# Moving half of the convolutions next to the next first product, and building the band matrices on TensorE, in a fused convolution and three-product kernel

## The chip, the cores and the metric

The kernel runs on one core of a Trainium2 chip. The metric is the device time of one execution in microseconds (us), taken as the median over several runs; less is better. Before the change it is 532.6 us (three runs, 532.53 to 532.73). One more execution was taken with the hardware profiler; all durations below that belong to single instructions come from it.

## The reference

A causal convolution over the sequence, with seven taps and one set of softmax weights for each of eight heads, feeds a gated product with four weight matrices:

```
# x: (8, 3904, 192), weight: (8, 7)
w = exp(weight - max) / (sum + 1e-9)            # softmax over the 7 taps of a head
x_pad = 6 rows of zeros, then x                 # for each of the 8 sequences
conv[b, s, h, :] = sum_k w[h, k] * x_pad[b, s + k, h, :]     # 24 columns a head
x2 = conv.reshape(31232, 192)
a, b = x2 @ w1, x2 @ w2                         # 192 x 1024 each
out = ((a * b) @ w3) @ w_out                    # 1024 x 1024, 1024 x 192
```

Since nothing stands between the last two products, the kernel multiplies w3 by w_out once (1024 x 192) and uses that as the weight of its second product.

## The kernel before

The 31232 tokens are two streams of 15616 tokens (`NS = 2`, index r). A stream is worked off in 31 rounds of 512 tokens (`CH`, `NR`), the last of 256.

**Convolution.** Tokens are cut into windows of 64 rows, which give 58 results each (`Q`, `ST`), and windows into ten blocks of 10 to 36 windows (`SIZES`). `load_x` brings a block's rows to the tile xb by DMA from GpSimd's queue, stream 0 on partitions 0 to 63 and stream 1 on 64 to 127. The convolution of a head is a product with a 64 x 64 band matrix whose seven diagonals hold the head's weights. `conv(b, h0, nh)` (L237) issues four matmuls of 64 x 64 tiles for each head (two halves of the block, two streams) into a PSUM buffer (tile cps, L254) and then moves the result to the tile convo (L271, or L428 in the prologue). `conv_two` (L480) calls it for two heads one by one, and after the last head of a block calls `store`, which writes convo to a scratch tensor in DRAM (rows, from SP's queue); `send` then issues transposing DMAs from rows to xT, also on SP. xT is a ring of four rounds. The first three blocks do not go through DRAM: TensorE transposes them (`pe_transpose`, tile tps, L307).

**Band matrices.** `band_of` takes the matrix of a head from the tile Aband, [128, 2, 2, 2, 64]: two groups g of four heads, a direct and a swapped half, two heads, 64 columns. Each needs its values on the partitions of either stream. Before the change, `band(g)` (L204) builds them on VectorE: a mask cmask with a one at every place of each of eight diagonals, made by GpSimd (L151), times the weights wsb (L206), then three additions that sum over the eight (L213 twice, L216); `band_swap` (L219) copies the two partition halves crosswise with VectorE and ScalarE.

**First product.** `first_product(R)` (L345) goes over eight column tiles ft of the 1024 columns. For each, six matmuls for a (pa) and six for b (pb), in pairs that use either half of the rows of the array (L360); ScalarE copies pa to asb (L366) and VectorE multiplies asb by pb into the tile abT (L367). Because x of the two streams lies on either partition half, the weights are needed on both halves: wn as loaded (`load_w`, in two column parts) and wsw with the halves exchanged (`swap_w`, L334, three column parts `WC`: 0 to 511, 512 to 767, 768 to 1023). Column tiles 0 to 3 use part 0, 4 and 5 part 1, 6 and 7 part 2.

**Second product.** `second_product(R, r)` (L372) has 32 matmuls of 128 x 192 (tile ops, L378); ScalarE empties it (osb, L383) and SP sends it to the output.

**Order.** The order on every engine is the one in which the code issues (`manual_schedule`). All PSUM tiles come in turn from four buffers of two banks each (tag banks), so a tile waits until the tile four before it has been emptied. The prologue (L425 to L462) makes the bands, the convolution of block 0 and its transposes, and the swapped weights. Then come the first products of rounds 0, 1 and 2 with the convolutions of blocks 1 and 2 in between (L470 to L478), the product of w3 and w_out with block 3 (L491), and the steady phases (L507). Phase p runs the first products of two rounds (phase 0: none), and the second products of two earlier rounds, `done` and `done + 1`, r = 0 and r = 1 each. A block has two phases; in each, `conv_two` runs twice, once between the two second products of each round, with both evictions on VectorE. GpSimd reloads x for the next block inside the phase, behind a small copy (pace) that waits for a first product. `warm` (L171) issues matmuls on zeros at the start.

Of the kernel before, what the change touches and what calls it, by code (L numbers as in the profile page):

```python
# [8 lines left out]

FP32 = mybir.dt.float32  # L10
BF16 = mybir.dt.bfloat16
AX = mybir.AxisListType
ALU = mybir.AluOpType
# [4 lines left out]
def kernel(  # L18
# [10 lines left out]
    nc = tc.nc  # L29

    B, S, D = x.shape
    H, K = weight.shape
# [1 line left out]
    DFF = moe_w1.shape[1]  # L34
    JT = DFF // 128
    PAD = K - 1
    KP = 8
    assert K <= KP

    NS = 2  # L40
    TS = B * S // NS
# [4 lines left out]
    Q = 64  # L46
# [7 lines left out]
    NB = len(SIZES)  # L54
# [14 lines left out]
    def banks(name):  # L69
        return psum.tile([128, NS, CH], FP32, tag="banks", name=name)  # L70
# [4 lines left out]
    def slot(shape, dtype, name):  # L75
        return stage.tile(shape, dtype, tag="slot", bufs=5, name=name)
# [68 lines left out]

    ones = const.tile([128, 1], BF16)
    nc.gpsimd.memset(ones, 1.0)
    cmask = const.tile([128, Q, KP], BF16)
    for r in range(NS):
        ps = slice(Q * r, Q * r + Q)  # L150
        nc.gpsimd.affine_select(  # L151
            out=cmask[ps], in_=ones[ps].unsqueeze(2).to_broadcast([Q, Q, KP]),
            pattern=[[-1, Q], [-1, KP]], compare_op=ALU.is_equal,
            fill=0.0, base=0, channel_multiplier=1)
    wn = [const.tile([128, DFF], BF16, name=f"wn{k}", tag=f"wn{k}") for k in range(3)]
    wsw = [const.tile([128, DFF], BF16, name=f"ws{k}", tag=f"ws{k}") for k in range(3)]

# [2 lines left out]
    def load_w(c0, c1):  # L160
        cs = slice(c0, c1)
        nc.gpsimd.dma_start(out=wn[0][:, cs], in_=moe_w1[0:128, cs])
        nc.gpsimd.dma_start(out=wn[2][0:Q, cs], in_=moe_w1[128:192, cs])
        nc.gpsimd.dma_start(out=wn[2][Q:128, cs], in_=moe_w2[128:192, cs])
        nc.gpsimd.dma_start(out=wn[1][:, cs], in_=moe_w2[0:128, cs])

    load_w(0, WC[2])
    ident = const.tile([128, 128], BF16)
    make_identity(nc, ident)

    def warm(n, t=None):  # L171
        t = banks("warm") if t is None else t
        for j in range(n):
            nc.tensor.matmul(t[:, j % 2, :], zeros[:, 0:128], zeros, start=True, stop=True)  # L174

    warm(28)


    wmax = const.tile([128, H], FP32)
    wsum = const.tile([128, H], FP32)  # L180
    wsb = const.tile([128, 2, 2, KP], BF16)
    nc.vector.memset(wsb, 0.0)  # L182
    nc.vector.reduce_max(out=wmax, in_=wall, axis=AX.X)
    nc.vector.tensor_tensor(
        out=wall, in0=wall, in1=wmax.unsqueeze(2).to_broadcast([128, H, K]), op=ALU.subtract)
# [3 lines left out]
    for r in range(NS):  # L189
        ps = slice(Q * r, Q * r + Q)  # L190
        nc.vector.tensor_tensor(
            out=wsb[ps, :, :, 0:K],
            in0=wall[ps].rearrange("p (g a e) k -> p g a e k", g=2, a=2)[:, :, r],
            in1=wsum[ps].rearrange("p (g a e) -> p g a e", g=2, a=2)[:, :, r].unsqueeze(3)
                .to_broadcast([Q, 2, 2, K]),
            op=ALU.mult)
# [4 lines left out]
        g, j, e = h // 4, (h % 4) // 2, h % 2  # L201
        return Aband[Q * r:Q * r + Q, g, int(j != r), e, :]

    def band(g):  # L204
        c = slot([128, 2, Q, KP], BF16, "cprod")
        nc.vector.tensor_tensor(  # L206
            out=c,
            in0=cmask.unsqueeze(1).to_broadcast([128, 2, Q, KP]),
            in1=wsb[:, g].unsqueeze(2).to_broadcast([128, 2, Q, KP]),
            op=ALU.mult)  # L210
        n = KP // 2
        while n > 1:
            nc.vector.tensor_tensor(out=c[:, :, :, 0:n], in0=c[:, :, :, 0:n],  # L213
                                    in1=c[:, :, :, n:2 * n], op=ALU.add)
            n //= 2
        nc.vector.tensor_tensor(out=Aband[:, g, 0], in0=c[:, :, :, 0], in1=c[:, :, :, 1],  # L216
                                op=ALU.add)

    def band_swap(g, half, f):  # L219
        d, e = ((Q, 0), (0, Q))[half]  # L220
        f(out=Aband[d:d + Q, g, 1], in_=Aband[e:e + Q, g, 0])


    xT = [const.tile([128, RING], BF16, name=f"xT{k}", tag=f"xT{k}") for k in range(NP)]
# [12 lines left out]
    def conv(b, h0, nh, evict=None, lead=0):  # L237
        n = SIZES[b] // 2
        if h0 == 0:
            convo_of[b] = work.tile([128, n, NP, NS, Q], BF16, tag="convo", bufs=2, name="convo")  # L240
        convo = convo_of[b]
        cps = banks("cps")
        warm(lead, cps)
        wd = nh * G

        def view(ps, r):
            return cps[ps, r, 0:n * wd].rearrange("p (w g) -> p w g", g=wd)

        for j in range(nh):
            h = h0 + j  # L250
            for c in range(2):
                xb, w0 = xb_of[b][c]
                for r in range(NS):
                    nc.tensor.matmul(  # L254
                        view(slice(Q * c, Q * c + Q), r)[:, :, j * G:(j + 1) * G],
                        band_of(h, r),
                        xb[Q * r:Q * r + Q, w0:w0 + n, h * G:(h + 1) * G],
                        start=True, stop=True)
        src = cps[:, :, 0:n * wd].rearrange("p r (w g) -> p r w g", g=wd)
        o, moves = 0, []  # L260
        for k, c0, m in segments(h0 * G, wd):
            moves.append((convo[:, :, k, :, c0:c0 + m].rearrange("p w r g -> p r w g"),
                          src[:, :, :, o:o + m]))
            o += m
        if h0 + nh == H:
            del xb_of[b]
        if evict == ():
            return moves
        for e, (dst, part) in enumerate(moves):
            f = evict or [nc.scalar.copy]  # L270
            f[e % len(f)](out=dst, in_=part)  # L271
# [28 lines left out]
    def pe_transpose(b, k, lead=0):  # L300
        n = SIZES[b] // 2
        convo = convo_of[b]
        tps = banks_bf16("tps")
        for w in range(lead):
            nc.tensor.transpose(out=tps[:, w % 2, :], in_=zeros[:, 0:128], identity=ident)
        for w in range(n):
            nc.tensor.transpose(  # L307
                out=tps[:, w, :],
                in_=convo[:, w, k].rearrange("p r g -> p (r g)"), identity=ident)
        t0 = tok(FIRST[b])  # L310
        dst = xT[k][:, t0:t0 + 2 * n * ST].rearrange("p (c w s) -> p c w s", c=2, w=n)
        src = tps[:, 0:n, :].rearrange("p w (c s) -> p c w s", c=2)
        return dst, src[:, :, :, 0:ST]
# [20 lines left out]
    def swap_w(k, part, engines):  # L334
        cs = slice(WC[part], WC[part + 1])
        for f, (d, e) in zip(engines, ((0, Q), (Q, 0))):
            f(out=wsw[k][d:d + Q, cs], in_=wn[k][e:e + Q, cs])
# [89 lines left out]
    def move(f, pair):  # L427
        f(out=pair[0], in_=pair[1])  # L428

    band(0)  # L430
    band_swap(0, 0, V)
    band_swap(0, 1, A)
    band(1)
    band_swap(1, 0, V)
    m0, m1 = conv(0, 0, 4, ())
    move(A, m0)
    band_swap(1, 1, A)
    move(V, m1)
    t0 = pe_transpose(0, 0, 10)
    swap_w(0, 0, (V, A))  # L440
    for m in conv(0, 4, 2, ()):
        move(V, m)
    for m in conv(0, 6, 2, ()):
        move(A, m)
    move(V, t0)
    swap_w(2, 0, (V, A))
    t1 = pe_transpose(0, 1, 8)
    move(V, t1)
    t2 = pe_transpose(0, 2)
    move(A, t2)  # L450
    swap_w(1, 0, (V, A))
    for k in (0, 2, 1):
        swap_w(k, 1, (P, V))
    load_w(WC[2], WC[3])
    load_x(2)
    for k in (0, 2, 1):
        swap_w(k, 2, (P, P))
    load_wo()
# [5 lines left out]
    def seq(*fs):  # L464
        def run():
            for f, *a in fs:
                f(*a)
        return run

    first_product(0, lead=2, between={  # L470
        2: seq((conv, 1, 0, 4)),
        3: seq((conv, 1, 4, 4)),
        6: seq((pe_transposes, 1))})
    first_product(1, {
        0: seq((conv, 2, 0, 4)),
# [4 lines left out]
    def conv_two(b, h, engines):  # L480
        for j, f in enumerate(engines):
            conv(b, h + j, 1, (f,))
        if h + 2 == H:
            store(b)

    def send(last):
        while sent[0] <= last and min((sent[0] + 1) * CH, TS) <= stored[0]:
            transposes(sent[0])
            sent[0] += 1
# [16 lines left out]
    done = 0  # L506
    for p, rounds in enumerate(phases):  # L507
        b, e = PROLOGUE_BLOCKS + p // 2, p % 2
        if b < NB:
            for xb, r, w in zero_rows.pop(b, []):  # L510
                nc.gpsimd.memset(xb[Q * r:Q * r + PAD, w, :], 0.0)
        for j, R in enumerate(rounds):
            first_product(R)
            if j == 0 and b + 1 < NB:
                P(out=pace, in_=abT_of[R][0:1, JT - 1, 1, 0:2])  # L515
                load_x(b + 1, (0, 1) if p == 1 else (e,))
        last = NR if p == len(phases) - 1 else done + 2
        for i in range(done, last):
            second_product(i, 0)
            if b < NB and i < done + 2:  # L520
                conv_two(b, 4 * e + 2 * (i - done), (V, V))
            second_product(i, 1)
        done = last
        send(min(NR - 1, LAG + 2 * p + 4))
    assert sent[0] == NR

# [29 lines left out]
```

## Time and profile before

| what | us |
|---|---|
| median of 3 runs | 532.6 |
| the profiled execution | 533.68 |
| its span on the core, first to last instruction | 532.0 |
| first matmul of the first product | 14.02 |
| all abT multiplies (L367), 248 of them | 298.4 |
| all copies to asb (L366) | 247.6 |
| all conv evictions on VectorE (L271), 65 | 52.0 |
| GpSimd busy in the whole span | 53.0 |

A line of the chain of waits has a start, a length and the instructions on it: it is followed back from the last instruction to whatever released each step. In a line of the timeline or of the groups, "x" is the number of instructions, the times are start and length (timeline) or the union and the mean of one (groups), and the brackets hold the idle time before and what ended it. PE is TensorE, PEld its weight loads, DVE VectorE, ACT ScalarE, POOL GpSimd, SP SyncE. A matmul's own length is modelled and overlaps with the next one's, so the distance between starts is what a matmul costs.

### The profile page before, as it was taken

How to read it: one execution, taken by the hardware profiler on the slowest of the kernel's cores; microseconds unless marked ns; L12 is line 12 of the kernel's file. 1: busy time of each engine (PE TensorE's matmuls, PEld its weight loads, DVE VectorE, ACT ScalarE, POOL GpSimd, SP SyncE). 2: the span in 40 equal slices, each digit the busy share in tenths (PEclk: the TensorE clock that was granted, in tenths of full speed). 3: DMA queues.
4: the chain of work that ended last, by engine and by line, in shares of the span. 5: the costliest groups of instructions: out<-in, count | busy, mean ns of one | idle time of the engine just before them, and what ended most of it. 6: DMA issues, size and time to landing. Idle time of an engine off the chain costs nothing.

```text
span 532.0 us, 12708 instructions
## 1 busy us (share of the span) xinstructions
PE 524.0 (98%) x5469; PEld 339.3 (64%) x5469; DVE 363.1 (68%) x350; ACT 317.4 (60%) x350; POOL 53.0 (10%) x95
## 2 busy tenths in 40 slices
PE   8999999999999999999999999999999999999995
PEld 4455874846658476584765757557575674847685
DVE  6779459578594875949669496784957849286560
ACT  3888647375573755737467374664746647375552
POOL 8851002002010100201001010020000000000000
PEclk9999999999999999999999999999999999999998
DMA  7999457989473694637956468655624065240203
GB/s 101 141 206 182 93 96 171 206 175 125 132 99 99 154 144 129 88 103 156 137 139 78 130 150 128 118 66 145 136 80 120 1 172 106 90 76 31 90 22 130
DMA packets 130541, 63.13 MB, mean 119 GB/s; under 512 B 83352, under 2 KB 129460, under 8 KB 130484
## 3 DMA queue, kind: packets, MB, share of 16 engines
q1 hardware_dynamic: 91764, 45.65, 35.7%
q0 software_dynamic: 38576, 16.63, 26.3%
q8 instruction: 43, 0.70, 0.6%
q14 instruction: 14, 0.11, 0.1%
q10 hardware_dynamic: 144, 0.03, 0.0%
HBM read 33.28 MB, written 34.82 MB: 128 GB/s over the span
## 4 chain that ended last, share of the span: by engine, by line
PE 94%; DVE 3%; ACT 1%; DMA 1%; issue 0%; ACTq 0%; DVEq 0%
PE ops L378 31%; PE pa L360 30%; PE pb L360 29%; PE cps L254 2%; DVE abT L367 1%; PE wps L418 1%; ACT asb L366 1%; DMA wall<-in_weight_dram 1%; PE tps L307 1%; PE w3ps L409 0%; DVE cprod L213 0%; DVE cprod L206 0%; DVE Aband L216 0%; DVE convo L428 0%; DVE w3T L412 0%
## 5 line engine op out<-in xcount | busy, mean ns | idle before, releaser
L367 DVE TENSOR_TENSOR abT<-asb,pb 128x1024 bf16<-128x1024 bf16 (+1 forms) x248 | 298.4, 1204 | 77.0 <-ACT asb L366 60.5
L366 ACT CAST asb<-pa 128x1024 bf16<-128x1024 f32 (+1 forms) x248 | 247.6, 999 | 64.1 <-PE pa L360 63.4
L360 PE MATMUL pb<-xT,wn 64*128 64x512 bf16 (+1 forms) x744 | 199.7, 373 | 0.2
L360 PE MATMUL pa<-xT,wn 64*128 64x512 bf16 (+1 forms) x744 | 197.8, 373 | 0.4
L360 PE MATMUL pa<-xT,ws 64*128 64x512 bf16 (+1 forms) x744 | 197.9, 373 | 0.0
L360 PE MATMUL pb<-xT,ws 64*128 64x512 bf16 (+1 forms) x744 | 195.7, 373 | 0.0
L360 PEld LDWEIGHTS <-wn 64*128 64x128 bf16 x1488 | 138.3, 94 | 84.6 <-issue 2.6
L360 PEld LDWEIGHTS <-ws 64*128 64x128 bf16 x1488 | 130.3, 94 | 72.0 <-issue 1.4
L378 PEld LDWEIGHTS <-abT 128*128 128x128 bf16 x1952 | 159.1, 98 | 13.8 <-issue 13.8
L378 PE MATMUL ops<-W_sb,abT 128*128 128x192 bf16 x1952 | 167.8, 246 | 0.0
L383 ACT COPY osb<-ops 128x768 f32<-128x768 f32 (+1 forms) x62 | 48.9, 789 | 134.1 <-PE ops L378 134.1
L271 DVE CAST convo<-cps 128x864 bf16<-128x864 f32 (+7 forms) x65 | 52.0, 847 | 66.7 <-PE cps L254 66.7
L111 POOL DMA_DIRECT2D xb<-in_x_dram x38 | 29.9, 797 | 12.2 <-DMA w3b<-in_moe_w_dram 5.2
L515 POOL COPY pace<-abT 1x2 bf16<-1x2 bf16 x9 | 1.6, 176 | 269.7 <-DVE abT L367 269.7
L254 PE MATMUL cps<-xb,Aband 64*64 64x432 bf16 (+3 forms) x320 | 17.8, 309 | 0.2 <-DVE abT L367 0.2
L174 PE MATMUL warm<-zeros 128*128 128x512 bf16 x28 | 8.9, 491 | 1.4 <-DVE wsb L182 1.4
L254 PEld LDWEIGHTS <-Aband 64*64 64x64 bf16 x320 | 5.8, 105 | 6.8 <-issue 5.7
L271 ACT CAST convo<-cps 128x640 bf16<-128x640 f32 (+4 forms) x13 | 7.4, 606 | 0.8 <-PE cps L254 0.8
L174 PEld LDWEIGHTS <-zeros 128*128 128x128 bf16 x30 | 3.4, 119 | 6.5 <-issue 3.6
L418 PE MATMUL wps<-wo_b,w3T 128*128 128x192 bf16 x64 | 6.3, 246 | 0.1
L418 PEld LDWEIGHTS <-w3T 128*128 128x128 bf16 x64 | 5.1, 98 | 1.0 <-issue 1.0
L409 PE MATMUL w3ps<-ident,w3b 128*128 128x128 bf16 x64 | 4.6, 219 | 0.0
(55 smaller groups left out, 64.3 us busy)
## 6 DMA issues: line engine op xcount, KB each, us to landing
out_dram<-osb SPq DMA_DIRECT2D x60, 384.0 KB, 2.9
xb<-in_x_dram POOLq DMA_DIRECT2D x14, 432.0 KB, 8.9
rows<-convo SPq DMA_DIRECT2D x7, 648.0 KB, 7.5
xb<-in_x_dram POOLq DMA_DIRECT2D x8, 384.0 KB, 9.9
w3b<-in_moe_w_dram POOLq DMA_DIRECT2D x8, 256.0 KB, 8.8
rows<-convo SPq DMA_DIRECT2D x3, 576.0 KB, 8.4
xT<-rows SPq DMA_TRANSPOSE x84, 2.7
rows<-convo SPq DMA_DIRECT2D x2, 540.0 KB
```

Source lines behind the costliest of these rows:

```text
L111: nc.gpsimd.dma_start(out=xb[Q * r:Q * r + Q, w:w + m, :], in_=x_spans(r, i, m))
L174: nc.tensor.matmul(t[:, j % 2, :], zeros[:, 0:128], zeros, start=True, stop=True)
L254: nc.tensor.matmul(view(slice(Q * c, Q * c + Q), r)[:, :, j * G:(j + 1) * G], band_of(h, r), xb[Q * r:Q * r + Q, w0:w0 + n, h * G:(h + 1) ...
L271: f[e % len(f)](out=dst, in_=part)
L307: nc.tensor.transpose(out=tps[:, w, :], in_=convo[:, w, k].rearrange("p r g -> p (r g)"), identity=ident)
L360: nc.tensor.matmul(p[:, r, 0:N], w_of(i, k, r)[rs, ft * 128:(ft + 1) * 128], xT[k][rs, r0:r0 + N], start=(k == 0), stop=(k == NP - 1))
L366: nc.scalar.copy(out=asb[:, :, 0:N], in_=pa[:, :, 0:N])
L367: nc.vector.tensor_tensor(out=ab[:, ft, :, 0:N], in0=asb[:, :, 0:N], in1=pb[:, :, 0:N], op=ALU.mult)
L378: nc.tensor.matmul(ops[:, g // 2, (g % 2) * D:(g % 2) * D + D], ab[:, jt, r, g * 128:(g + 1) * 128], W_sb[:, jt, :], start=(jt == 0), stop ...
L383: nc.scalar.copy(out=osb.rearrange("p (a g) d -> p a (g d)", g=2), in_=ops[:, 0:ng // 2, 0:2 * D])
L409: nc.tensor.transpose(out=tps[:, gt, :], in_=w3b[:, gt * 128:(gt + 1) * 128], identity=ident)
L418: nc.tensor.matmul(wps[:, 0, 0:D], w3T[:, gt, :], wo_b[:, gt, :], start=(gt == 0), stop=(gt == JT - 1))
```

## The change

Three edits go together.

In the steady phases, `conv_two` stays between the two second products of the first of the two rounds; the other call goes behind all four second products, directly ahead of the next phase's first product. The last phases, which have no block left, are as before.

The bands are made in another way. GpSimd makes a plain identity with 64 further columns that continue it (identw: columns 64 to 191 are an identity with its halves exchanged), and one diagonal strip of 70 columns on each partition half (diag) in place of cmask. `band_taps(g)` multiplies seven overlapping views of the strip, each shifted by one column, by the weights, one multiply on VectorE with the columns innermost; `band_sum(g)` sums the seven on TensorE, with the identity for the direct and the exchanged identity for the swapped half, and one copy from PSUM fills Aband[:, g]. wsb has seven entries in place of eight and is no longer cleared first.

The prologue is reordered: 18 warm matmuls in place of 28; no dummy transposes; convs of two heads; `swap_w` of part 0 for k = 0 and 2, and of parts 1 and 2 for all three, by GpSimd alone (before: part 0 by VectorE and ScalarE, part 1 by GpSimd and VectorE, part 2 by GpSimd); `load_w` of columns 768 to 1023 and `load_x(2)` between the swaps. In round 0 the second conv of block 1 goes from behind column tile 3 to behind column tile 4.

```diff
-    cmask = const.tile([128, Q, KP], BF16)
-    for r in range(NS):
-        ps = slice(Q * r, Q * r + Q)
+    identw = const.tile([128, 128 + Q], BF16)
+    diag = const.tile([128, Q + PAD], BF16)
+    for m in (identw[:, 0:128], identw[:, 128:128 + Q], diag[0:Q], diag[Q:128]):
+        p, n = m.shape
         nc.gpsimd.affine_select(
-            out=cmask[ps], in_=ones[ps].unsqueeze(2).to_broadcast([Q, Q, KP]),
-            pattern=[[-1, Q], [-1, KP]], compare_op=ALU.is_equal,
-            fill=0.0, base=0, channel_multiplier=1)
+            out=m, in_=ones[0:p].to_broadcast([p, n]), pattern=[[-1, n]],
+            compare_op=ALU.is_equal, fill=0.0, base=0, channel_multiplier=1)
+    ident, swapped = identw[:, 0:128], identw[:, Q:Q + 128]
...
-    ident = const.tile([128, 128], BF16)
-    make_identity(nc, ident)
...
-    warm(28)
+    warm(18)
...
-    wsb = const.tile([128, 2, 2, KP], BF16)
-    nc.vector.memset(wsb, 0.0)
+    wsb = const.tile([128, 2, 2, K], BF16)
...
-    def band(g):
...
-    def band_swap(g, half, f):
...
+    d0 = diag[:, 0:1]
+    taps = bass.AP(tensor=d0.tensor, offset=d0.offset,
+                   ap=[list(d0.ap[0]), [0, 2], [1, K], [1, Q]])
+
+    def band_taps(g):
+        c = slot([128, 2, K, Q], BF16, "cprod")
+        nc.vector.tensor_tensor(
+            out=c, in0=taps, in1=wsb[:, g].unsqueeze(3).to_broadcast([128, 2, K, Q]),
+            op=ALU.mult)
+        return c
+
+    def band_sum(g, c, f):
+        bps = banks("bps")
+        for v, lhsT in enumerate((ident, swapped)):
+            out = bps[:, 0, v * 128:v * 128 + 128].rearrange("p (e s) -> p e s", e=2)
+            for k in range(K):
+                nc.tensor.matmul(out, lhsT, c[:, :, k, :], start=(k == 0), stop=(k == K - 1))
+        f(out=Aband[:, g].rearrange("p v e s -> p (v e s)"), in_=bps[:, 0, 0:256])
...
-    band(0)
-    band_swap(0, 0, V)
-    band_swap(0, 1, A)
-    band(1)
-    band_swap(1, 0, V)
-    m0, m1 = conv(0, 0, 4, ())
-    move(A, m0)
-    band_swap(1, 1, A)
-    move(V, m1)
-    t0 = pe_transpose(0, 0, 10)
-    swap_w(0, 0, (V, A))
-    for m in conv(0, 4, 2, ()):
-        move(V, m)
-    for m in conv(0, 6, 2, ()):
-        move(A, m)
-    move(V, t0)
-    swap_w(2, 0, (V, A))
-    t1 = pe_transpose(0, 1, 8)
-    move(V, t1)
-    t2 = pe_transpose(0, 2)
-    move(A, t2)
+    c0, c1 = band_taps(0), band_taps(1)
+    band_sum(0, c0, A)
+    band_sum(1, c1, V)
+    for h, f in ((0, V), (2, A), (4, V), (6, A)):
+        for m in conv(0, h, 2, ()):
+            move(f, m)
+    swap_w(0, 0, (P, P))
+    swap_w(2, 0, (P, P))
+    load_w(WC[2], WC[3])
+    for k, f in ((0, V), (1, A), (2, V)):
+        move(f, pe_transpose(0, k))
     swap_w(1, 0, (V, A))
+    load_x(2)
     for k in (0, 2, 1):
-        swap_w(k, 1, (P, V))
-    load_w(WC[2], WC[3])
-    load_x(2)
+        swap_w(k, 1, (P, P))
     for k in (0, 2, 1):
         swap_w(k, 2, (P, P))
...
         2: seq((conv, 1, 0, 4)),
-        3: seq((conv, 1, 4, 4)),
+        4: seq((conv, 1, 4, 4)),
...
             second_product(i, 0)
-            if b < NB and i < done + 2:
-                conv_two(b, 4 * e + 2 * (i - done), (V, V))
+            if b < NB and i == done:
+                conv_two(b, 4 * e, (V, V))
             second_product(i, 1)
         done = last
+        if b < NB:
+            conv_two(b, 4 * e + 2, (V, V))
         send(min(NR - 1, LAG + 2 * p + 4))
```

Here V, A and P are copies by VectorE, ScalarE and GpSimd, and `move` empties one PSUM piece.

More of the change, by code (lines that the diff above doesn't have):

```diff
@@ L6 @@
 from concourse import bass_utils, mybir
-from concourse.masks import make_identity
 from concourse._compat import with_exitstack
@@ L36 @@
     PAD = K - 1
-    KP = 8
-    assert K <= KP
     NS = 2
@@ L191 @@
         nc.vector.tensor_tensor(
-            out=wsb[ps, :, :, 0:K],
+            out=wsb[ps],
             in0=wall[ps].rearrange("p (g a e) k -> p g a e k", g=2, a=2)[:, :, r],
@@ L202, in band_of @@
         return Aband[Q * r:Q * r + Q, g, int(j != r), e, :]
-    def band(g):
-        c = slot([128, 2, Q, KP], BF16, "cprod")
+    d0 = diag[:, 0:1]
[3 more added lines that the diff above has]
+        c = slot([128, 2, K, Q], BF16, "cprod")
         nc.vector.tensor_tensor(
-            out=c,
-            in0=cmask.unsqueeze(1).to_broadcast([128, 2, Q, KP]),
-            in1=wsb[:, g].unsqueeze(2).to_broadcast([128, 2, Q, KP]),
+            out=c, in0=taps, in1=wsb[:, g].unsqueeze(3).to_broadcast([128, 2, K, Q]),
             op=ALU.mult)
[L211 to L217, printed above, removed]
-    def band_swap(g, half, f):
-        d, e = ((Q, 0), (0, Q))[half]
-        f(out=Aband[d:d + Q, g, 1], in_=Aband[e:e + Q, g, 0])
+        return c
[6 more added lines that the diff above has]
+        f(out=Aband[:, g].rearrange("p v e s -> p (v e s)"), in_=bps[:, 0, 0:256])
     xT = [const.tile([128, RING], BF16, name=f"xT{k}", tag=f"xT{k}") for k in range(NP)]
```

## The prediction

> **What bounds the kernel now.** I read the page's busy shares and chain shares first, then the chain of waits in order of time at the start and in one steady phase, then the timeline of the other engines at those places.
>
> ```profile
> PE 524.0 (98%) x5469; PEld 339.3 (64%) x5469; DVE 363.1 (68%) x350; ACT 317.4 (60%) x350; POOL 53.0 (10%) x95
> PE 94%; DVE 3%; ACT 1%; DMA 1%; issue 0%; ACTq 0%; DVEq 0%
> ```
>
> TensorE holds 94% of the chain that ends last. So a change pays in two ways only: it lets the first real product start earlier, or it takes time out of TensorE's own row of work. The chain at the start (start us, length us, what):
>
> ```profile
> 6.74 0.70 DVE cprod L206
> ...
> 9.00 0.83 DVE cprod L206
> ...
> 10.74 0.64 DVE Aband L216
> ...
> 11.63 0.49 DVE convo L428
> ...
> 12.90 0.76 PE tps L307 x10
> 13.65 0.43 PE pa L174 x2
> 14.09 0.75 PE pa L360 x6
> 14.84 1.01 PE pb L360 x6
> ```
>
> VectorE builds both bands (6.74 to 11.60) while TensorE spins on zeros; the first product starts at 14.09, and its first pb takes 1.01 instead of the 0.65 of every later one, because ScalarE is still copying swapped weights. One steady phase:
>
> ```profile
> 94.34 0.65 PE pb L360 x6
> 94.99 2.75 PE ops L378 x32
> 97.73 0.49 PE cps L254 x8
> 98.22 5.39 PE ops L378 x64
> 103.61 0.49 PE cps L254 x8
> 104.10 2.75 PE ops L378 x32
> 106.84 0.75 PE pa L360 x6
> ```
>
> Nothing but TensorE is in it. 32 ops matmuls that follow their own kind take 2.64 (the piece at 62.41 of the same chain); behind a first product or a conv they take 2.75, and 64 take 5.39, which is 5.28 + 0.11. Six pa after pb take 0.65, after ops 0.75. Each change of kind costs 0.10 to 0.11. The timeline around it has the evictions:
>
> ```profile
> 97.77 0.80 ACT L383 COPY osb<-ops 128x768 f32<-128x768 f32 x1 [2.38 <-PE ops L378]
> 98.09 2.09 DVE L271 CAST convo<-cps 128x864 bf16<-128x864 f32 x3 [1.44 <-PE cps L254]
> 103.97 2.02 DVE L271 CAST convo<-cps 128x864 bf16<-128x864 f32 x2 [3.79 <-PE cps L254]
> ```
>
> VectorE empties two convs in 2.0 to 2.1 us, behind second products that don't need it. GpSimd at the start:
>
> ```profile
> 4.25 2.21 POOL L151 TENSOR_SCALAR_AFFINE_SELECT cmask<-ones 64x512 bf16<-64x512 bf16 x2
> ...
> 17.13 2.65 POOL L337 COPY ws<-wn 64x256 bf16<-64x256 bf16 x6 [0.45 <-DMA wn<-in_moe_w_dram]
> ```
>
> **The steady phases.** In the twelve phases that have a conv (p = 0 to 11) the second conv_two goes behind the last second product, against the next first product. Before, from the first ops to the end of the first pa: 2.75 + 0.49 + 5.39 + 0.49 + 2.75 + 0.75 = 12.62. After: 2.75 + 0.49 + 0.11 + 3 x 2.64 + 0.49 + pa. A pa behind a conv took 0.75 where it didn't wait (chain, 20.66) and 0.82 where it did (18.85). With 0.75 the sum is 12.51: one change of kind fewer, 0.11 a phase, 1.3 in twelve. With 0.82 it is 0.04 a phase, 0.5.
>
> What hid the moved evictions is gone: they now stand on VectorE ahead of the next abT multiply. Counted from the first conv matmul's start (97.66 in the timeline), they end 2.52 later (98.09 + 2.09). The four PSUM buffers go round as ops, ops, cps, cps, pa, pb, pa, pb, so the second pb takes the second cps. It wants to start at 0.56 + 0.75 + 0.65 + 0.65 = 2.61. The first abT could start when ScalarE's copy of the first pa ends, 0.56 + 0.75 + 1.01 = 2.32, and now starts at about 2.55 and ends at 3.77 (1.22 each); the third pb, which needs its buffer, starts at 3.91. The cover holds by about 0.1 us, and grows, since abT takes 1.22 to 1.24 and a pa with pb 1.295. The first pb needs the last osb gone: 0.9 against 1.31. I take off 0.1 in all for phases whose evictions come in three pieces: **1.2**. Ends 0 (0.1 lost in every phase) and 1.3.
>
> On SP, store moves behind the out of the last second product, so rows are written about 2.6 us later and the transposes behind them too. They were issued at 114.43 (x6, 9.9 us) for rounds that start at 139.5: 15 us of cover; without it the 2.6 would show in full, once per block. On GpSimd nothing waits for the moved conv but the reload of its xb, a phase later.
>
> **The prologue.** wsb is ready at 6.64 as before (the memset of wsb was off the path, at 1.28). Removed on VectorE: two L206 (0.69, 0.82), four L213 (0.43, 0.41 twice), two L216 (0.38, 0.63), two swaps (0.19). Added: two taps multiplies of 896 elements each, which the trace doesn't show. Ends: by L206 (1024 in 0.69, both operands contiguous) 0.61; by abT (1024 in 1.22, the slowest full multiply) 1.07. The weight is now one value held for 64 elements; L216, whose operands aren't contiguous either, takes 0.51 for 128, far worse per element than L206. So I take 1.07: taps at 6.74 to 7.83 and 7.86 to 8.95.
>
> The Trainium skill, "Vector Engine (DVE) Microarchitecture Reference", section 5.1, speaks against this multiply: two 16-bit results a cycle need an innermost step of one, and one element read again and again by a two-source operation ran at one a cycle. By it the multiply is an estimated 0.93 plus a fixed part, by L206 alone 0.61, which would bring the sum below 0.28 earlier.
>
> TensorE: 18 warm matmuls instead of 28. They start 0.427 apart up to 6.49 and 0.216 apart from 6.85 on, so the eighteenth starts at 7.71 and band_sum(0) can start at 7.93. Its 14 matmuls of 128 columns, by w3ps (8 in 0.45), take 0.056 each: last start 8.65, done at 8.87. Band_sum(1) waits for the taps, 9.0 to 9.95. ScalarE empties the first (256 columns, by 320 in 0.43: 0.38), VectorE the second (by 320 in 0.49: 0.41), done at 10.38. Convs of two heads start at 9.88, 10.0, 10.42 and 10.5, done 0.33 later. xb landed early: the convs before ran at 10.18 straight off the warm matmuls.
> VectorE: heads 0-1 (480 columns, 0.66) to 11.07, heads 4-5 (0.49 + 0.31) to 11.85. ScalarE: heads 2-3 (0.30 + 0.43) to 11.07, heads 6-7 (0.56) to 11.66. Transposes at 11.15, 11.65 and 11.92, five each. Moves to xT: VectorE 0.44 to 12.30, ScalarE 0.64 to 12.76, VectorE to 12.84. Two warm matmuls (0.43) fit in between; pa starts at 12.62 against 14.02 of its first matmul. ScalarE's half of ws1 (0.62) ends at 13.40, so pb still waits 0.16, and the second pa starts at 13.9 instead of 15.48: **1.55**. Ends 0.6 (0.1 more at each of ten hand-overs) and 1.85 (taps at 0.61).
>
> GpSimd: four selects of 128, 64, 70 and 70 elements replace two of 512 (1.08 each) and the later identity (0.20 + 0.29). By the identity's 0.29 for 128 they take about 0.95, so the four weight loads issue 1.2 earlier (5.2 instead of 6.41), land near 8.9 to 11.4, and x of block 1 goes out at 7.45. It takes over four 64x512 copies: no row, 0.40 to 0.80 by 64x256, I take 0.80. They run from 9.0 to 12.3; the last operand of the first pa needs them at 13.06. Then the second loads and x of block 2 issue (3.8, to 16.1), against 16.7 before; six 64x256 copies (2.65) to 18.75, six more to 21.4. Their readers come at 18.35 (fifth pa; its pb, which reads the last copied, 19.0) and 21.4 to 22.05. Cover 0.3 to 0.7 us. Output weights and w3 leave 1.7 later; the last w3 landed at 36.0 and is used past 50.
>
> Conv (1, 4..7) goes from behind the fourth pa/pb to behind the fifth. Same pieces, and the waits of 0.1 to 0.2 that follow each conv in these rounds stay: 0, ends -0.2 and 0.2.
>
> **Sum.** 1.2 + 1.55 = 2.75. The profiled execution took 533.68 (span 532.0), 1.1 above the median 532.6; I take the difference off the median: **529.85 us**, and 530.9 for an execution like the profiled one. Less than 0.2%, 1.07 us, can't be told from no change.
>
> **Rivals.**
> (a) GpSimd is late with the swapped weights: 64x512 copies at 1.2 instead of 0.8 put the sixth copy of the second part at 20.3, 1.3 behind its pb, and the gain falls to 1.45: 531.15. For: cover of only 0.3, nothing like it measured. Against: the 0.40 of 64x256 held at 17.13 beside a busy VectorE.
> (b) TensorE slows down again. 18 dummy transposes and ten warm matmuls are gone, and the trace shows that it starts slow (0.427 apart for 5 us). A relapse of 2.5 to 5 us at half speed loses 1.3 to 2.5, say 1.7: 531.55. Against: from 7.93 to 12.4 no gap is above 0.4.
> (c) Slower: the moved evictions hold up the abT multiplies. One place, the head of each of twelve first products. It decides from 2.75/12 = 0.23 us a phase beyond the 0.1 of cover, evictions of 2.4 instead of 2.1. At 0.4 a phase net of everything it costs 4.8 and takes the 1.2 away: 532.6 - 1.55 + 4.8 = 535.85. Against: at 2.02 and 2.09 they fit, and abT behind them has 0.05 to spare in every round of buffers.
> (d) The steady phases give nothing (0.82 for pa, or small waits), only the prologue stays: 531.05.
>
> **Chances.** Forecast 0.60; (d) 0.14, (a) 0.10, (b) 0.09, (c) 0.07. Faster by more than 0.2% (under 531.53): forecast, (d), (a) and part of (b), 0.82; within: 0.11, rest of (b) and half-way (c); slower 0.07. The range goes from both upper ends with a little over (1.3 + 1.85 + 0.2 = 3.35: 529.25, and 0.2 for the measurement) to 531.7, past (a), (b) and (d).
>
> **What would show it.** The first pa near 12.6 in the chain; two taps multiplies of 1.07; steady phases that go ops, cps, ops x96, cps, pa in 12.51; no idle VectorE or TensorE time at the second and third pb of a round; fifth and sixth pb of round 0 without a wait for ws. Wrong would be matmuls 0.43 apart after 8 us, a pa or pb that waits for convo or abT, or a phase of 32.68 us as before (65.54 to 98.22).

## The result, and the profile after

530.35 us, median of 6 runs (530.2 to 530.57), against 532.57 for the kernel before (6 runs, 532.37 to 532.73): 0.9959 of the time, 95% interval 0.9946 to 0.9971. That is 2.2 us less; 529.85 was predicted. Held against the kernel before once more, in the second group of runs below, the same kernel took 530.78 (ratio 0.9963, 0.9951 to 0.9976).

The profiled execution took 530.57 (span 528.9). The page, busy shares and chain shares:

```profile
PE 521.7 (99%) x5469; PEld 351.0 (66%) x5469; DVE 359.3 (68%) x337; ACT 316.2 (60%) x348; POOL 54.8 (10%) x102
PE 96%; DVE 2%; ACT 1%; issue 0%; ACTq 0%
```

The chain at the start (start us, length us, what; lines after L35 are three to sixteen lower than before):

```profile
1.39 6.95 PE warm L170 x18
8.33 1.58 PE bps L215 x28
...
9.94 0.42 DVE Aband L216
10.36 0.57 DVE convo L423
...
11.07 1.12 PE tps L302 x15
12.19 0.43 PE pa L170 x2
12.62 0.76 PE pa L355 x6
13.37 0.73 PE pb L355 x6
```

The first pa comes at 12.62 instead of 14.09 and the first pb takes 0.73 instead of 1.01. VectorE's multiplies and additions for the bands are gone from the chain (one copy, L216, is left); in their place stand the matmuls on zeros and the band sums. The chain of a steady phase, from its second products on:

```profile
92.62 0.65 PE pb L355 x6
93.27 2.75 PE ops L373 x32
96.01 0.49 PE cps L249 x8
96.50 8.03 PE ops L373 x96
104.53 0.49 PE cps L249 x8
105.02 0.75 PE pa L355 x6
105.77 0.65 PE pb L355 x6
106.42 0.65 PE pa L355 x6
107.06 0.72 PE pb L355 x6
```

From the first ops to the end of the first pa it is 105.77 - 93.27 = 12.50, to be held against 12.62 before: one change of kind less, as the sum had it. But the second pb, at 107.06, takes 0.72 instead of 0.65, and in the phase before that (74.35) 0.79. These two lengths alternate over ten phases and nothing else in these phases differs. The last two phases with a conv, whose block is smaller (720 columns in place of 864), have no such wait.

Where the time came from, by the same event in both profiled executions (starts in us, from the chain; the last row is the end of the span):

| event | before | after | gained by then |
|---|---|---|---|
| first pa | 14.09 | 12.62 | 1.47 |
| second pa | 15.85 | 14.10 | 1.75 |
| first ops | 62.41 | 60.66 | 1.75 |
| first pa of phase 1 | 74.16 | 72.30 | 1.86 |
| last phase's ops | 513.33 | 511.32 | 2.01 |
| end of the span | 532.0 | 528.9 | 3.1 |

So in these two executions the prologue gave 1.75 and all steady phases together 0.26, of which 0.2 is the last two phases with a conv (32.46 in place of 32.56 each). The last 1.1 is no gain: behind the last osb copy (0.48 from 526.72 and 524.71) the profiled execution of before takes 4.8 us to its end and that of after 3.7, in which only the last output transfers land. In the profiles of the twelve other runs this end takes 3.6 to 4.1, so the 4.8 is the exception; it fits the 1.1 by which the profiled execution of before lies above its median.

### The profile page after: what moved, and what is told of

Same layout as the page of the kernel before. It is cut to its first block, busy times and chain, and to the rows that moved or that the text cites. A ratio compares the mean times of both kernels' runs of the same rounds, so it can differ in the third digit from the quotient of the medians.

```text
span 528.9 us, 12698 instructions
## 1 busy us (share of the span) xinstructions
PE 521.7 (99%) x5469; PEld 351.0 (66%) x5469; DVE 359.3 (68%) x337; ACT 316.2 (60%) x348; POOL 54.8 (10%) x102
## 4 chain that ended last, share of the span: by engine, by line
PE 96%; DVE 2%; ACT 1%; issue 0%; ACTq 0%
PE ops L373 31%; PE pa L355 30%; PE pb L355 29%; PE cps L249 2%; PE warm L170 1%; DVE abT L362 1%; ACT asb L361 1%; PE wps L413 1%; PE tps L302 1%; PE w3ps L404 0%; PE bps L215 0%; ACT convo L266 0%; DVE w3T L407 0%; DVE convo L423 0%; ACT osb L378 0%
## 5 line engine op out<-in xcount | busy, mean ns | idle before, releaser
L355 PE MATMUL pb<-xT,wn 64*128 64x512 bf16 (+1 forms) x744 | 201.8, 372 | 0.2
L355 PEld LDWEIGHTS <-ws 64*128 64x128 bf16 x1488 | 129.0, 94 | 68.4 <-issue 3.3
L373 PE MATMUL ops<-W_sb,abT 128*128 128x192 bf16 x1952 | 165.7, 246 | 0.0
L170 PE MATMUL warm<-zeros 128*128 128x512 bf16 x18 | 6.9, 572 | 1.4 <-DVE zeros L140 1.4
L332 POOL COPY ws<-wn 64x256 bf16<-64x256 bf16 (+1 forms) x16 | 7.2, 449 | 0.9
```

The costliest lines, as they stand in the source:

```text
L355: nc.tensor.matmul(p[:, r, 0:N], w_of(i, k, r)[rs, ft * 128:(ft + 1) * 128], xT[k][rs, r0:r0 + N], start=(k == 0), stop=(k == NP - 1))
L373: nc.tensor.matmul(ops[:, g // 2, (g % 2) * D:(g % 2) * D + D], ab[:, jt, r, g * 128:(g + 1) * 128], W_sb[:, jt, :], start=(jt == 0), stop ...
```

## Experiments

The kernel before ran beside each group at 532.53 to 532.60 in the median. Every kernel below is the changed one with one edit, unless it says otherwise.

**One edit alone, and without it.** steady_only is the kernel before with the steady edit; prologue_only is the changed kernel with the conv pairs back in both rounds:

```diff
-            if b < NB and i == done:
-                conv_two(b, 4 * e, (V, V))
+            if b < NB and i < done + 2:
+                conv_two(b, 4 * e + 2 * (i - done), (V, V))
             second_product(i, 1)
         done = last
-        if b < NB:
-            conv_two(b, 4 * e + 2, (V, V))
```

> The kernel before with the steady edit alone (the second conv pair of each phase behind the last second product). Theory (the second pb of the next first product waits for the buffer of the second conv, 0.14 us where the pair's evictions come in three pieces and 0.07 where they come in two, so that a phase gains almost nothing): 0.27 us less than before, 532.3, and those waits in the trace. Rival (the cover holds as predicted, 1.2 us from the phases, and the prologue gave less): 531.4 and no waits.

> The changed kernel with the conv pairs back between the second products, so the prologue edits alone. Theory (nearly all of the gain is the prologue's): 530.6, first ops at 60.7 in the chain, phases of 32.69. Rival (the phases give 1.2): 531.55.

Measured: steady_only 532.3 (ratio to before 0.9995, 0.9986 to 1.0004), prologue_only 530.68 (0.9968, 0.9956 to 0.9979). The parts add up, 0.25 and 1.87, though the 0.25 alone can't be told from nothing (its interval holds 1). In the trace of steady_only the second pb at 75.95 takes 0.78 although its prologue is the old one; so the wait belongs to the steady edit. prologue_only has phases of 32.69 us and no such wait. The prediction's 1.2 for the phases was not there.

**What the second pb waits for.** VectorE's timeline of the changed kernel behind the first conv pair (the conv's first matmul starts at 71.74):

```profile
72.17 2.09 DVE L266 CAST convo<-cps 128x576 bf16<-128x576 f32 x3 [6.42 <-PE cps L249]
74.17 2.48 DVE L362 TENSOR_TENSOR abT<-asb,pb 128x1024 bf16<-128x1024 bf16 x2
```

and TensorE's:

```profile
71.74 0.56 PE L249 MATMUL cps<-xb,Aband 64*64 64x432 bf16 x8
...
72.23 0.39 PE L355 MATMUL pa<-xT,wn 64*128 64x512 bf16 x1
...
72.89 0.38 PE L355 MATMUL pb<-xT,wn 64*128 64x512 bf16 x1
...
73.54 0.59 PE L355 MATMUL pa<-xT,ws 64*128 64x512 bf16 x2
73.76 0.59 PE L355 MATMUL pa<-xT,wn 64*128 64x512 bf16 x2
73.97 0.38 PE L355 MATMUL pa<-xT,ws 64*128 64x512 bf16 x1
74.31 0.37 PE L355 MATMUL pb<-xT,wn 64*128 64x512 bf16 x1
```

Pairs of matmuls start 0.216 apart, so the pb could have started at 74.19; it starts at 74.31, behind the evictions' end at 72.17 + 2.09 = 74.26. To show that it is this eviction, two kernels divide the eviction of the last conv between VectorE (stream 0) and ScalarE (stream 1). The first:

```diff
-            conv(b, h + j, 1, (f,))
+            if f is None:
+                for dst, part in conv(b, h + j, 1, ()):
+                    V(out=dst[:, 0], in_=part[:, 0])
+                    A(out=dst[:, 1], in_=part[:, 1])
+            else:
+                conv(b, h + j, 1, (f,))
...
-            conv_two(b, 4 * e + 2, (V, V))
+            conv_two(b, 4 * e + 2, (V, None))
```

> The changed kernel, but the eviction of the last conv ahead of a first product is split: stream 0 by VectorE, stream 1 by ScalarE, which is idle for 0.45 us there. Theory (the wait of the second pb is for that eviction): the waits go in ten phases, 5 x (0.14 + 0.07) = 1.05 less, 529.3, phases of about 32.58. Rival (the wait is for something else, or ScalarE's later copy of the first pa puts a new one at the third pb): 530.35 or more.

Measured: 541.93 (ratio 1.0177, 1.0163 to 1.0191), 9.4 us slower than before. ScalarE's timeline says why:

```profile
72.06 0.80 ACT L378 COPY osb<-ops 128x768 f32<-128x768 f32 x1 [1.84 <-PE ops L373]
74.06 0.52 ACT L469 CAST convo<-cps 128x432 bf16<-128x432 f32 x1 [1.19 <-DVE convo L468]
74.47 1.94 ACT L361 CAST asb<-pa 128x1024 bf16<-128x1024 f32 x2
```

In the built program ScalarE's half waits for VectorE's (the line's own releaser, L468), although it reads the other half of the buffer. It stood until VectorE, last in its own queue, had done its half (74.03), and the copy of the first pa stood behind it: it started at 74.47, where its pa had ended near 73.3. Ten phases took 33.62 to 33.69, 0.97 more than in the changed kernel, and the last two 0.8 to 0.9 more. The expectation was wrong, but the run gives a price to the prediction's rival (c): here the copy of the first pa came some 1.15 late, and almost all of it was paid, once a phase.

The second kernel has the two lines in the other order, so that ScalarE's half runs in its idle 0.45 us and is long done when VectorE comes to its own:

```diff
-                    V(out=dst[:, 0], in_=part[:, 0])
-                    A(out=dst[:, 1], in_=part[:, 1])
+                    A(out=dst[:, 1], in_=part[:, 1])
+                    V(out=dst[:, 0], in_=part[:, 0])
```

> The changed kernel, with the eviction of the last conv ahead of a first product split again, but with ScalarE's half first (stream 1, in its idle 0.45 us) and VectorE's half behind it, so that neither waits long for the other. Theory (the second pb waits for that eviction alone): it ends near +2.1 us instead of +2.5, the waits of 0.14 and 0.07 go, phases of 32.58, 1.05 less than the changed kernel. Rival (ScalarE's copy of the first pa, pushed back, puts a new wait at the third pb): no less, or more.

Measured: 529.56 (ratio to before 0.9941, 0.9928 to 0.9953), against 530.78 for the changed kernel in the same group. VectorE's timeline and the chain:

```profile
71.92 1.12 DVE L266 CAST convo<-cps 128x576 bf16<-128x576 f32 x2 [6.42 <-PE cps L249]
72.96 0.60 DVE L469 CAST convo<-cps 128x432 bf16<-128x432 f32 x1
73.89 2.52 DVE L362 TENSOR_TENSOR abT<-asb,pb 128x1024 bf16<-128x1024 bf16 x2 [0.33 <-ACT asb L361]
```

```profile
73.46 0.65 PE pa L355 x6
74.10 0.65 PE pb L355 x6
```

The evictions end at 73.56, ahead of the pb, which takes 0.65; VectorE even waits 0.33 for ScalarE. Every full phase takes 32.58, by 0.11 less than before the change: what the prediction had asked of the move. Between the same two events of the chain, first ops and last phase's ops, the split takes 1.03 off the changed kernel, where 1.05 was expected.

**The prologue's parts.**

> The changed kernel itself, so that the other runs here can be held against it on one chip. 530.35, 2.2 less than before; the first pa between 11.5 and 12.6, by when TensorE's clock is released and by when the head weights land.

530.78 (530.31 to 531.08), first pa's first matmul at 12.08. band_dve makes the bands as before (L204 to L221 and the mask of the kernel before), the rest as changed; swap_va gives part 0 of two swapped weights back:

```diff
-    swap_w(0, 0, (P, P))
-    swap_w(2, 0, (P, P))
+    swap_w(0, 0, (V, A))
+    swap_w(2, 0, (V, A))
```

> The changed kernel with its bands made as before (mask of 512 columns by GpSimd, products and additions and swaps on VectorE and ScalarE), all else kept. Theory (the chain over VectorE is what the new bands shorten): VectorE is busy with bands to 11.6 and the evictions follow, the first pa comes about 1.0 later, 1.0 more than the changed kernel. Rival (the order and GpSimd's swaps gave the gain): less than 0.3 more.

> The changed kernel with the swapped weights of part 0, k = 0 and 2, copied by VectorE and ScalarE as before, in the place where GpSimd does it now. Theory (they stood on the path of the moves to xT and of the first pb): ScalarE's two copies of 0.62 push its move to xT and its copy of ws1, 0.7 to 1.2 more than the changed kernel. Rival (they fit into waits): less than 0.3 more.

band_dve took 533.72 (ratio to before 1.0023, 1.0013 to 1.0032): 2.9 more than the changed kernel, three times the expectation, and slower than before the change. Its chain runs over GpSimd:

```profile
4.25 1.09 POOL cmask L150
...
5.38 1.09 POOL cmask L150
...
6.53 0.81 POOL identw L156
7.33 0.56 POOL wn L167
...
8.42 4.79 DMA wn<-in_moe_w_dram
...
13.26 0.62 POOL ws L340
13.89 1.46 PE pa L363 x6
15.35 1.04 PE pb L363 x6
```

The masks hold up the weight loads (the first issues at 7.29, in the changed kernel at 5.21), these the swaps, and the first pa and pb wait for them. So, by this trace, the diagonal strip does not just save VectorE work: it is what makes the swaps on GpSimd affordable. What the bands on TensorE would be worth with GpSimd's queue kept short was not tried.

swap_va took 530.96, 0.2 more than the changed kernel, which those two medians can't tell apart (530.78 to 531.25 against 530.31 to 531.08). Its profile shows ScalarE's two copies in the chain and the second pa at 14.79, against 14.10 in the profile of the changed kernel, whose zeros end at the same time. So where they are on the path they cost 0.7, at the lower end of the theory; how often they are there stays open.

**The conv that went one column tile on.**

```diff
-        4: seq((conv, 1, 4, 4)),
+        3: seq((conv, 1, 4, 4)),
```

> The changed kernel with the second conv of block 1 back behind column tile 3 of round 0. Prediction's step: 0, ends -0.2 and 0.2, so 530.2 to 531.0 with the changed kernel at 530.35 to 530.8. Rival (GpSimd's later swaps of part 1 make the fifth pb wait, and the conv behind tile 3 gave them time): the distance from the first pa to the first ops, 47.94 in the changed kernel, shrinks; or it grows because ScalarE has two conv evictions in a row.

530.53, and by matmul starts 47.95 us from the first pa to the first ops against 47.94: worth nothing, as predicted.

**The matmuls on zeros.** In the profile of the changed kernel they end at 8.33 on the chain although the first taps multiply is done at 7.55. `warm(18)` was tried with 16, 14 and, on top of the split eviction, 20 and 14:

> The changed kernel with 16 matmuls on zeros at the start in place of 18. Theory (they end after the first taps multiply, so they, not VectorE, hold up band_sum(0), and band_sum(1) then waits for its taps at 8.6): 0.3 less, 530.05, first pa at 12.3. Rival 1 (the clock of TensorE needs them): matmuls 0.43 apart in the band sums, slower by 0.5 or more. Rival 2 (another step of the prologue bounds): 530.35.

> The changed kernel with 14 matmuls on zeros in place of 18, one step beyond 16, whose runs spread from 530.2 to 531.9. Theory (the clock of TensorE is released at a time of its own, 4.8 to 6.9 us in the traces so far, and the band sums behind fewer zeros fall before it more often or it comes later): slower than the changed kernel by 0.4 or more in the median, a wide spread, some band sums 0.107 apart. Rival (only the end of the zeros counts): at or below the changed kernel's 530.35 to 530.8.

> The split eviction with ScalarE first, 529.56, with 20 matmuls on zeros in place of 18. If their end is on the path as in the trace of the changed kernel, 0.43 more: 530.0. If what counts is that the clock is released before the band sums, 529.6 or less and a smaller spread.

> The split eviction with ScalarE first (529.5) and 14 matmuls on zeros in place of 18. Theory (the first pa waits for the taps, no longer for the zeros, whenever the clock is released late): 0.0 to 0.4 less than with 18, 529.1 to 529.5, the fastest of all kernels here. Rival (the zeros were never on the path in most executions): 529.5.

Measured: 16: 531.13 (530.21 to 531.89); 14: 530.23 (529.85 to 530.24); split with 20: 529.46 (529.21 to 529.79); split with 14: 529.51 (529.38 to 530.16). There is no order in these by the number of zeros, so neither the theory of a late clock nor that of a late end is borne out by the medians; no trace has band sums 0.107 apart. With 14 the chain is the one of the prediction's working, over the landing of the head weights (3.89), both taps multiplies and the second band sum.

The traces show one reason why fewer zeros don't pay: the first product then waits for the weights that GpSimd swaps. GpSimd's line in the runs with 16, and with the split and 14:

```profile
9.46 2.59 POOL L332 COPY ws<-wn 64x512 bf16<-64x512 bf16 x4 [0.58 <-DMA wn<-in_moe_w_dram]
```

```profile
11.47 1.28 POOL L332 COPY ws<-wn 64x512 bf16<-64x512 bf16 x2 [1.29 <-DMA wn<-in_moe_w_dram]
```

GpSimd itself stood waiting for a weight load to land. With 16 the first pa started at 11.38 of the chain, 0.77 ahead of the changed kernel's second profile (12.15), in which the head weights landed as early. But it took 1.11 in place of 0.75 and the fifth pb 0.93 in place of 0.65, and the first ops came only 0.26 earlier (59.93 against 60.19). With the split and 14 the two took 0.99 and 0.93. How late the loads land differs from profile to profile. The runs with 16 spread over 1.7 us: in two of the eight, some 1.1 and 1.3 of it lie outside the core's span (531.89 with a span of 529.1, 531.72 with 528.7; the others have 1.7 to 1.9 outside it). What spread the rest stays open.

The fastest kernels are the three with the split eviction in ScalarE's order, 529.46 to 529.56; they can't be told apart.

## Why the prediction was right, and where it was off

**The prologue** (1.55 predicted; 1.75 by the second pa, and 1.87 in the run with it alone) had its costs about right, but not, in this execution, the wait on which its path turned. The first matmul of pa started at 12.55 (predicted 12.62). The taps multiplies took 1.09 and 1.08 (predicted 1.07, by the abT row and not by L206):

```profile
6.46 2.09 DVE L205 TENSOR_TENSOR cprod<-diag,wsb 128x896 bf16<-128x896 bf16 x2
9.94 0.42 DVE L216 CAST Aband<-bps 128x256 bf16<-128x256 f32 x1 [1.39 <-PE bps L215]
```

The Trainium skill's rule in "Vector Engine (DVE) Microarchitecture Reference", section 5.1, that an element read again and again keeps such a multiply at one result a cycle, agrees: 896 in 1.09, where 1024 with contiguous operands took 0.69. The path differs in two places. The weights were ready at 6.34 instead of 6.64 (see the last section), so the second taps multiply ended at 8.55 and not 8.95. The zeros ended later than I had them, since in this execution the step from 0.427 to 0.216 apart came later, and the band sums started at 8.17 in place of 7.93 and ran in one piece to 9.9. So band_sum(1) did not wait for its taps, as the working had it: the zeros set the time. The two misses cancel, and that 12.55 lies so close to 12.62 is luck. In the profile of prologue_only, which has the same start-up, the zeros ended earlier, the chain ran over the taps, and pa started at 12.18. The second pa gained 0.2 more than predicted: 0.07 came with the first pa, and 0.09 because pb waited 0.07 and not 0.16.

**GpSimd** (rival a) had more room than I gave it. A 64x512 copy took 0.61, not 0.80, and the timeline shows its queue early:

```profile
4.25 0.48 POOL L149 TENSOR_SCALAR_AFFINE_SELECT identw<-ones 128x128 bf16<-128x128 bf16 x2
4.69 0.58 POOL L149 TENSOR_SCALAR_AFFINE_SELECT diag<-ones 64x70 bf16<-64x70 bf16 x2
5.21 0.60 POOL L160 DMA_DIRECT2D wn<-in_moe_w_dram  x1
...
9.05 2.59 POOL L332 COPY ws<-wn 64x512 bf16<-64x512 bf16 x4
...
15.29 5.31 POOL L332 COPY ws<-wn 64x256 bf16<-64x256 bf16 x12
```

Part 0 was done at 11.64 (predicted 12.3) and all swaps at 20.6 (21.4). No pa or pb waited for them there. The rival was real all the same. In band_dve, where the loads issue 2.1 later on that queue, it decides. In the profiles of three other kernels with the new start-up, a weight load landed later and the fifth pb waited for its swapped weights, as the rival had it: 0.07 in prologue_only, 0.28 with 16 zeros and with the split and 14.

**The steady phases** (1.2 predicted, 0.26 measured) are the step that failed, and in it one number: "Counted from the first conv matmul's start ... It wants to start at 0.56 + 0.75 + 0.65 + 0.65 = 2.61". The 0.56 is 98.22 of the chain less 97.66 of the timeline, but the chain puts a conv's or an ops' step some 0.07 later than its start, and a pb's some 0.17. So the 0.75 of the first pa, a step of the chain, is too long here as well: by starts it is 0.66 (72.23 to 72.89). By starts alone the conv takes 98.15 - 97.66 = 0.49, and the pb wants to start 0.49 + 0.66 + 0.65 + 0.65 = 2.45 after the conv. The evictions end at 2.52, and the pb starts 0.05 behind their end: the cover of 0.1 that the working had was a lack of 0.12, or of 0.06 where they come in two pieces. Measured on the chain: 0.14 and 0.07. With the saving of 0.11 unchanged the measured waits leave -0.03 and +0.04 a phase, in turn, which is the 32.72 and 32.65 of the traces against 32.69 before. The mechanism (a change of kind less, evictions ahead of the abT multiplies) and the 0.11 were right, and the split eviction shows that the 1.2 was to be had. Only the sign of the slack was wrong.

Rival (d), phases that give nothing, thus came true for the phases, and the prologue's 0.2 more made up for part of it: 2.2 in place of 2.75. Rival (b), a relapse of the clock, is not in any trace: band sums are 0.056 apart throughout. Rival (c) came true in kind and not in size: the moved evictions did hold up a pb, the sign of being wrong that the prediction had named, by 0.14 and 0.07 in ten phases; split_evict shows a hold-up at the same place at full price.

The 1.1 between the profiled execution and the median was rightly left out of the gain: it lay behind the last computation.

## What to carry to other kernels

Slack is a difference of two times, so both must come from one view: a chain's steps lay 0.07 to 0.17 us behind the timeline's starts here, as much as the slack itself. Where an eviction moves ahead of work that needs its buffer, look for an engine with an idle stretch at that very place and give it a share, and let its share come first where the program makes one reader of a tile wait for the other. When several edits of a start-up go together, ask of each queue what it still holds for the next one: here a shorter mask on GpSimd paid for the copies that were moved there.

## What the runs showed of the hardware

**VectorE and GpSimd hold each other up.** L184 (two operands in SBUF, 56 elements) took 0.39 before the change, beside a GpSimd select that ended when it did, at 5.34. The same instruction took 0.22 in band_dve (L187), where it ran from 4.03 to 4.25, ahead of the first select. In band_dve, GpSimd's select of 128 columns took 0.81 beside VectorE's product of mask and weights (0.69), and 0.29 in the changed kernel, with no such VectorE instruction beside it. The Trainium skill, "SBUF — State Buffer", section "Who interferes with whom", says that a VectorE instruction with two SBUF inputs contends with a GpSimd instruction that reads SBUF, over a port that one of them locks; these rows agree that one waits for the other.

**TensorE's start.** The matmuls on zeros go from 0.427 to 0.216 apart at 4.8 to 7.3 us, differently in each profile, though they start at 1.39 in all. The granted clock reads 1.00 from the start in all of them, so it does not tell of this. The first pa of the changed kernel starts at 12.55 in one profile and at 12.08 in another, with nothing changed: the zeros end at 8.33 and 7.87 of the chain there. The head weights land at 3.8, 4.2 or 4.7, which counts only where the zeros end early enough for the chain to run over the taps.

**A change of kind on TensorE** costs 0.10 to 0.11 on the chain, from first to second product and back, and from a conv to either; a pa behind a conv costs no more (0.75) than a pa behind ops (0.75). What the change to a conv costs is within its 0.49 and was not taken apart.
